# Raw weight loads moved ahead of the chunk loads, scaled queries moved behind x, and weights prepared at three of five places

## The chip, the cores and the metric

The kernel runs on one core of one Trainium2 chip. The metric is the device time of one launch in microseconds (us). Besides TensorE (PE), which multiplies, the core has VectorE (DVE), ScalarE (ACT), GpSimd (POOL), and SyncE (SP), which here only issues transfers (DMAs) from memory. Each engine works through its instructions in program order; an instruction that waits holds up those behind it on its engine.

## The reference, cut to what matters

```python
# 1. decaying linear attention, blocks of 64 positions, 2 batches x 8 heads x 768 positions x 64
for b in range(nb):
    intra = (einsum('bhic,bhjc->bhij', qb, kb) * Dmask) @ vb
    inter = einsum('bhid,bhde->bhie', qb * lam_pow, kv_state)
    out[:, :, sl] = intra + inter
    kv_state = lam_block * kv_state + einsum('bhsd,bhse->bhde', kb * rev_pow, vb)
x = out.transpose(0, 2, 1, 3).reshape(1536, 512)
# 2. gated layer: d_model 512, d_ff 1536
xn = x / sqrt(mean(x * x) + 1e-06) * rms_g
g = xn @ w_gate
x = (silu(g) * (xn @ w_val)) @ w_out
# 3. maxout layer: d_ff 768
h = maximum(maximum(x @ w1, x @ w2), x @ w3)
return h @ w_out2
```

All numbers are 32-bit floats. A product of two matrices is made as three products of their high and low parts, so each weight is split once into `wh` and `wl`.

## The kernel before, in words

**Attention** goes by chunks of 128 positions, 12 in all (c = 0 to 11). A chunk passes through steps, each a letter: `T` (`turn`: transposes of k and q on PE into the banks `pk` and `pq`, copies `kT` and `qT` on ACT, and the scaled queries `qs` on DVE, which read `pq`), `K` or `k` (decayed keys `kd`, POOL), `C` (`scores`, PE), `a` and `b` (masked scores `A` and the states `S`, DVE), `V` (state, DVE), `M` (`mixed`: PE makes `px`, ACT its squares `sq` and the copy `x`), `U` (`summed`: PE `pm`, DVE `diag`, POOL the power), `N` (`normed`: PE `pb`, DVE `x`, ACT `xh`) and `R` (POOL `xl`). The strings in `orders` fix the order of the steps in a round; in round s step `T` works on chunk s, `C` on s-1, `M` on s-2, `N` on s-3. From chunk 5 on the squares are first added up on DVE (`zeros` in the rows, line 394), and `pm` reads that sum.

**Rounds 0 to 6** run by themselves, in the loop at the end of the program. From round 3 on each of them also prepares one weight.

**The first stage** (`first_stage`) then multiplies with the first four column blocks f = 0 to 3 of the gated layer, for three blocks j of 512 positions. Its unit of order is a **place**: each three matmuls of 128x512 are followed by one call of `spread`, which may run one third of a weight's preparation (`third_of_unit`) and some attention steps. `pg` and `pv` of one f have four places each, the sum over two f's (`out_two`, `acc`) eight. For j = 0: `pg` and `pv` of f = 0 are places 1 to 8, of f = 1 places 9 to 16, `pg` of f = 2 is 17 to 20, `out_two` over f = 0, 1 is 21 to 28, `pv` of f = 2 29 to 32, f = 3 33 to 40; then `pg` of the next block, 41 to 44, and `out_two` over f = 2, 3, 45 to 52.

**A weight's way.** One raw weight of 512 KB comes by DMA into a buffer `wraw` (`load_to`; one DMA for an out weight `o`, three for a gate `g` or value `v`). Then ACT makes `W` and shifts the low words (lines 252, 253), DVE makes `mid` twice and `W` (209, 212, 216), POOL adds the low words (219); a unit later ACT makes `wh` (180) and POOL `wl` (183). The raw buffers are few: of the first ten loads three in five use one of three buffers, the others one of two; the later ones all use the three. A load whose buffer is still being read waits on SP, and every load behind it waits too, since all of them stand in SP's one queue.

```python
if not lates and (pos["half"] - 1) % 4:      # spread: three places of four
    third_of_unit()
load_to(pos["raw"] + (3 if pos["half"] else 1))   # begin_unit
```

In the order of use the weights are g0, v0, g1, v1, g2, o0, o1, v2, g3, v3, o2, o3, and then g4, v4 and on, which the first stage doesn't need. Raw loads are counted from 0, so g4 is number 12 and v4 number 13.

**The second stage** does the rest of the gated layer and the maxout layer, with weights prepared at three of four gaps.

Of the kernel before, what the change touches and what calls it, by code (L numbers as in the profile page):

```python
# [9 lines left out]
F32 = mybir.dt.float32  # L10
# [8 lines left out]
P = 128  # L19
# [7 lines left out]
def tile_decay_attention_swiglu_maxout(  # L27
# [17 lines left out]
    B, H, S, D = q.shape  # L45
# [7 lines left out]
    C = P // 2  # L53
# [4 lines left out]
    NCH = NT // P  # L58
    CPNB = NB // P
# [9 lines left out]
    lates = []  # L69
# [161 lines left out]
    def begin_unit():  # L231
        if pos["made"] == len(unit_list):
            return
        key = unit_list[pos["made"]]
        at = group_of[key] % 2
        if first_use[key] <= pos["step"] + 6 and at < len(wpools) and (key is None or room[at]):
            pos["made"] += 1
            if key is None:
                stage1.append((None,) * 5)
                return  # L240
            room[at] -= 1
            held[key] = at
            if key[0][0] == "T":
                stage1.append((key, None if second_sum(key) else words[key[0][1], key[1]], at, None, None))
                return
            load_to(pos["raw"] + (3 if pos["half"] else 1))
            pos["raw"] += 1
            t = raws.pop(key).rearrange("p k (f w) -> p (k f) w", w=2)
            lo, hi = t[:, :, 0], t[:, :, 1]
            W = wp.tile([P, 512], I32, tag="W", name="W", bufs=4)  # L250
            words[key] = W
            nc.scalar.activation(out=W.bitcast(F32), in_=hi.bitcast(F32), func=AF.Abs)  # L252
            nc.scalar.activation(out=lo, in_=lo.bitcast(U32), func=AF.Copy, scale=2.0 ** -29)  # L253
            stage1.append((key, W, at, lo, hi))
# [32 lines left out]
        nc.gpsimd.tensor_tensor(out=kd[r], in0=qkv[c][0][r], in1=Tm[r, :, C - 1:C].to_broadcast([r.stop, H, D]),  # L287
                                op=ALU.mult)

    def turn(c):  # L290
        kn, qn, vn = qkv[c][0], qkv[c][1], qkv[c][2]
        pk = bank("pk")
        pq = bank("pq")
        pkv = pk.rearrange("p (a t) -> p a t", t=P)
        pqv = pq.rearrange("p (a t) -> p a t", t=P)
        for a in range(NP):
            nc.tensor.transpose(pkv[:, a, :], kn[:, 2 * a:2 * a + 2, :].rearrange("p h d -> p (h d)"), ident)
        for a in range(NP):
            nc.tensor.transpose(pqv[:, a, :], qn[:, 2 * a:2 * a + 2, :].rearrange("p h d -> p (h d)"), ident)
        kT = att.tile([P, NP, P], F32, tag="kT", name="kT", bufs=1)  # L300
        nc.scalar.copy(out=kT, in_=pkv)
        qT = att.tile([P, NP, P], F32, tag="qT", name="qT", bufs=1)
        nc.scalar.copy(out=qT, in_=pqv)
        qs = att.tile([P, NP, 2, C], F32, tag="qs", name="qs")
        h0 = 0 if c % CPB else 1
        nc.vector.tensor_tensor(
            out=qs[:, :, h0:], in0=pqv.rearrange("p a (h i) -> p a h i", h=2)[:, :, h0:],
            in1=lami.rearrange("p a (h i) -> p a h i", h=1).to_broadcast([P, NP, 2 - h0, C]), op=ALU.mult)
        if c == 0:
            decayed_keys(0)  # L310
        A = att.tile([P, H, C], F32, tag="A", name="A", bufs=1)
        st[c] = dict(kT=kT, qT=qT, qs=qs, vn=vn, A=A)

    def scores(c):
        d = st[c]
# [14 lines left out]
    def masked(hf):  # L330
        def piece(c):
            d = st[c]
            nc.vector.tensor_tensor(
                out=d["A"].rearrange("p (a t) i -> p t a i", t=2)[:, hf],
                in0=d["sc"][hf][:, :HF].rearrange("p (a i) -> p a i", i=C),
                in1=Tm.rearrange("p (a t) i -> p t a i", t=2)[:, hf], op=ALU.mult)
            if hf == 0:
                d["S0"] = last_state[0]
                d["S1"] = next_state(c, 0, d["S0"])
        return piece  # L340
# [82 lines left out]
    def rest(c):  # L423
# [5 lines left out]

    named = dict(M=(2, mixed), N=(3, normed), C=(1, scores), a=(1, masked(0)), R=(3, rest),  # L430
                 b=(1, masked(1)), U=(2, summed), V=(1, advance), T=(0, lambda c: (loads_at(c), turn(c))),
                 K=(-1, decayed_keys), k=(0, decayed_keys),
                 w=(3, lambda c: None))
    orders = ["MNCabUVTRK"] * (CPNB + 1) + ["MNCabUVTR", "MNCRabUkVT"] + ["MNCaUkRbVT"] * (NCH - CPNB - 2) + ["MNwRwU", "wwwNwR"]
    attn_q = [(s_, named[ch][1], s_ - named[ch][0]) for s_ in range(NCH + 3) for ch in orders[s_]
              if (ch == "K") <= s_ - named[ch][0] < NCH]
    gaps = [0, 0]
# [1 line left out]
    def attn_step():  # L439
        _, fn, c = attn_q.pop(0)  # L440
        fn(c)
# [16 lines left out]

    def spread():
        pos["half"] += 1  # L460
        if not lates and (pos["half"] - 1) % 4:
            third_of_unit()
        if gaps[0]:
            left = sum(1 for p in attn_q if p[0] <= gaps[1])
            for _ in range(-(-left // gaps[0])):
                attn_step()
            gaps[0] -= 1
            if not attn_q and not lates:
                att_ctx.close()
                wpools.append(ctx.enter_context(tc.tile_pool(name="wp2", bufs=8)))  # L470
                lates.append(ctx.enter_context(tc.tile_pool(name="late", bufs=1)))
                pos["narrow"] = False
                x_sums()
        if pos["half"] == 1:
            finish_unit(*stage2.pop(0))
            words_of_unit(3, *split_unit[0])
# [479 lines left out]
    with tc.manual_schedule():  # L956
        nc.scalar.dma_start(out=lam8, in_=lam.rearrange("(o h) -> o h", o=1).to_broadcast([P, H]))
        loads_to(0)
        for to, src in crosswise(g_sb, rms_g.rearrange("(a p) -> p a", p=P)):
            nc.scalar.dma_start(out=to, in_=src)  # L960
        make_identity(nc, ident)
        nc.vector.memset(ones, 1.0)
        nc.vector.memset(zeros, 0.0)
        nc.scalar.activation(out=mhalf, in_=zeros[:, 0:1], func=AF.Silu)
        nc.vector.memset(mhalf, -0.5)
        warm = bank("warm")
        for i in range(9):
            nc.tensor.matmul(out=warm[:, 0:P], lhsT=zeros, rhs=zeros, start=True, stop=True)
        nc.vector.tensor_tensor(out=diag, in0=ident[:, :C], in1=ident[:, C:], op=ALU.add)
        for hf in range(2):  # L970
            nc.vector.tensor_copy(out=lamh[64 * hf:64 * hf + 64, :],
                                  in_=lam8.rearrange("p (a t) -> p t a", t=2)[64 * hf:64 * hf + 64, hf, :])
        for a in range(NP):
            nc.vector.tensor_tensor_scan(
                out=lami[:, a, :], data0=lamh[:, a:a + 1].to_broadcast([P, C]), data1=zeros[:, :C],
                initial=1.0, op0=ALU.mult, op1=ALU.add)
        for h in range(H):
            nc.vector.tensor_tensor_scan(
                out=Tm[:, h, :], data0=lam8[:, h:h + 1].to_broadcast([P, C]), data1=diag,
                initial=0.0, op0=ALU.mult, op1=ALU.add)  # L980
        loads_to(1)
        pos["narrow"] = False
        unit_ = None
        for s_ in range(CPNB + 3):
            while attn_q[0][0] == s_:
                fn = attn_q[0][1]
                attn_step()
                if s_ > 2 and fn is named["N"][1]:
                    begin_unit()
                    unit_ = stage1.pop(0)  # L990
                if unit_ and s_ == CPNB + 2:
                    if fn is named["U"][1]:
                        words_of_unit(3, *added_later)
                    elif fn is named["V"][1]:
                        for n in range(3):
                            words_of_unit(n, *unit_, split_add=True)
                        split_unit.append(unit_)
                        stage2.append(unit_[:3])
                elif unit_ and fn is named["b"][1]:
                    words_of_unit(0, *unit_)  # L1000
                elif unit_ and fn is named["U"][1]:
                    words_of_unit(1, *unit_)
                    if stage2:
                        finish_unit(*stage2.pop(0))
                elif unit_ and fn is named["V"][1]:
                    words_of_unit(2, *unit_, split_add=s_ == CPNB + 1)
                    added_later = unit_
                    stage2.append(unit_[:3])
            if s_:
                load_to(pos["load"] + 1)  # L1010
        begin_unit()
        finish = first_stage()
        pos["step"] = len(steps)
        second_stage(finish)
# [31 lines left out]
```

## Time and profile before

| | |
|---|---|
| median of 3 runs | 547.11 us (546.27 to 547.93) |
| profiled execution | 548.3 us, of which the span is 546.5 us |
| PE busy | 531.0 us, 97% of the span |
| DVE, ACT, POOL busy | 371.7, 279.7, 300.9 us |
| DMA, first 110 us | 160 GB/s, DMA engines busy 64% |
| PE busy, first 110 us | 97.75 us |
| PE busy, from 110 us to 546 us | 433.27 of 436 us |

"Busy" is the sum of an engine's instructions. The granted TensorE clock is given as a share of full speed: 1.00 is 2.4 GHz, 0.5 is 1.2 GHz.

### The profile page before, as it was taken

How to read it: one execution, taken by the hardware profiler on the slowest of the kernel's cores; microseconds unless marked ns; L12 is line 12 of the kernel's file. 1: busy time of each engine (PE TensorE's matmuls, PEld its weight loads, DVE VectorE, ACT ScalarE, POOL GpSimd, SP SyncE). 2: the span in 40 equal slices, each digit the busy share in tenths (PEclk: the TensorE clock that was granted, in tenths of full speed). 3: DMA queues.
4: the chain of work that ended last, by engine and by line, in shares of the span. 5: the costliest groups of instructions: out<-in, count | busy, mean ns of one | idle time of the engine just before them, and what ended most of it. 6: DMA issues, size and time to landing. Idle time of an engine off the chain costs nothing.

```text
span 546.5 us, 9743 instructions
## 1 busy us (share of the span) xinstructions
PE 531.0 (97%) x3728; PEld 438.2 (80%) x3728; DVE 371.7 (68%) x680; ACT 279.7 (51%) x541; POOL 300.9 (55%) x247
## 2 busy tenths in 40 slices
PE   8998988999999999999999999999999999999997
PEld 7776756788888888888888888888888888888886
DVE  4776775545967676768677575887777477684464
ACT  3667674336264565464447426646466755651120
POOL 2485886241436486385556636886287544962050
PEclk9979999999999999999999999999999999999999
DMA  8888817000202132131221221121123222200015
GB/s 191 203 209 235 213 40 186 9 2 0 78 0 63 54 116 68 49 115 40 77 88 65 78 57 60 40 77 40 38 79 114 85 75 75 82 34 0 0 44 188
DMA packets 65598, 44.67 MB, mean 82 GB/s; under 512 B 40080, under 2 KB 61840, under 8 KB 65552
## 3 DMA queue, kind: packets, MB, share of 16 engines
q1 hardware_dynamic: 64848, 44.05, 28.4%
q8 instruction: 29, 0.48, 0.4%
q14 instruction: 17, 0.14, 0.1%
q10 hardware_dynamic: 704, 0.01, 0.1%
HBM read 40.90 MB, written 3.15 MB: 81 GB/s over the span
## 4 chain that ended last, share of the span: by engine, by line
PE 85%; DMA 4%; issue 2%; POOL 2%; SPq 2%; DVE 2%; ACT 2%; POOLq 0%; ACTq 0%; DVEq 0%
PE p L683 34%; PE acc L874 9%; PE r L683 8%; PE acc L480 6%; PE acc L482 6%; PE acc L481 6%; PE pv L490 5%; PE q L683 4%; PE pg L490 4%; DMA wraw<-in_moe_w_val_dram 3%; SPq L170 2%; PE px L377 1%; POOL W L219 1%; DMA qn<-in_q_dram 1%; PE sc L326 1%
## 5 line engine op out<-in xcount | busy, mean ns | idle before, releaser
L183 POOL TENSOR_TENSOR wl<-W,wh 128x512 fp32r<-128x512 f32 x77 | 100.7, 1309 | 60.5 <-ACT wh L180 60.5
L219 POOL TENSOR_TENSOR W<-W,wraw 128x512 int32<-128x512 int32 x60 | 80.6, 1343 | 71.9 <-DVE W L216 61.7
L180 ACT CAST wh<-W 128x512 fp32r<-128x512 f32 x77 | 47.8, 621 | 80.3 <-POOL W L219 78.8
L501 POOL TENSOR_TENSOR hl<-sg,hh 128x512 fp32r<-128x512 f32 x36 | 47.2, 1311 | 34.3 <-ACT hh L500 34.3
L683 PE MATMUL p<-xl,wh 128*128 128x512 f32 x148 | 57.6, 389 | 0.0
L683 PE MATMUL p<-xh,wl 128*128 128x512 f32 x148 | 57.6, 389 | 0.0
L683 PE MATMUL p<-xh,wh 128*128 128x512 f32 x148 | 57.6, 389 | 0.0
L480 PE MATMUL acc<-hh,wh 128*128 128x512 f32 x144 | 56.8, 394 | 0.7 <-DVE W L216 0.7
L481 PE MATMUL acc<-hl,wh 128*128 128x512 f32 x144 | 56.2, 390 | 0.0
L482 PE MATMUL acc<-hh,wl 128*128 128x512 f32 x144 | 56.1, 390 | 0.0
L252 ACT ACTIVATE W<-wraw 128x512 f32<-128x512 f32 x60 | 40.3, 672 | 9.9 <-DMA wraw<-in_moe_w_dram 4.4
L838 DVE TENSOR_TENSOR acc_sb<-acc,acc_sb 128x512 f32<-128x512 f32 x46 | 31.7, 690 | 19.5 <-PE acc L482 18.3
L209 DVE TENSOR_SCALAR mid<-W 128x512 f32<-128x512 f32 x58 | 39.8, 686 | 6.1 <-ACT W L252 6.1
L212 DVE TENSOR_SCALAR mid<-mid 128x512 int32<-128x512 int32 x58 | 40.3, 694 | 0.8
L216 DVE SCALAR_TENSOR_TENSOR W<-wraw,mid 128x512 int32<-128x512 int32 x58 | 39.5, 682 | 1.1
L253 ACT ACTIVATE wraw<-wraw 128x512 int32<-128x512 uint32 x60 | 39.9, 665 | 0.0
L738 ACT COPY c<-p 128x512 f32<-128x512 f32 x34 | 20.0, 587 | 38.3 <-PE p L683 38.3
L501 POOL TENSOR_TENSOR hl<-m,hh 128x512 fp32r<-128x512 f32 x18 | 24.2, 1350 | 23.0 <-ACT hh L500 23.0
L683 PE MATMUL p<-yl,wh 128*128 128x512 f32 x90 | 35.0, 389 | 0.0
L683 PE MATMUL p<-yh,wh 128*128 128x512 f32 x90 | 35.0, 389 | 0.0
L683 PE MATMUL p<-yh,wl 128*128 128x512 f32 x90 | 35.0, 389 | 0.0
L500 ACT CAST hh<-sg 128x512 fp32r<-128x512 f32 x36 | 22.3, 619 | 22.8 <-DVE sg L624 16.8
(176 smaller groups left out, 1322.9 us busy)
## 6 DMA issues: line engine op xcount, KB each, us to landing
wraw<-in_moe_w_out_dram SPq DMA_DIRECT2D x18, 512.0 KB, 3.4
wraw<-in_moe_w_dram SPq DMA_DIRECT2D x18, 512.0 KB, 3.5
kn<-in_k_dram SPq DMA_DIRECT2D x12, 256.0 KB, 4.3
qn<-in_q_dram SPq DMA_DIRECT2D x12, 256.0 KB, 4.7
vn<-in_v_dram SPq DMA_DIRECT2D x12, 256.0 KB, 4.9
wraw<-in_moe_w_gate_dram SPq DMA_DIRECT2D x12, 256.0 KB, 3.0
wraw<-in_moe_w_gate_dram SPq DMA_DIRECT2D x24, 128.0 KB, 3.3
wraw<-in_moe_w_val_dram SPq DMA_DIRECT2D x12, 256.0 KB, 3.0
```

The source lines that it names most:

```text
L180: nc.scalar.copy(out=wh, in_=W.bitcast(F32))
L183: nc.gpsimd.tensor_tensor(out=wl, in0=W.bitcast(F32), in1=wh.bitcast(F32), op=ALU.subtract)
L212: nc.vector.tensor_scalar(out=mid[key], in0=mid[key], scalar1=0x07FFFFFF, scalar2=3, op0=ALU.bitwise_and, op1=ALU.logical_shift_left)
L219: nc.gpsimd.tensor_tensor(out=W, in0=W, in1=lo, op=ALU.add)
L252: nc.scalar.activation(out=W.bitcast(F32), in_=hi.bitcast(F32), func=AF.Abs)
L480: nc.tensor.matmul(out=out, lhsT=wh, rhs=xh_, start=first, stop=False)
L481: nc.tensor.matmul(out=out, lhsT=wh, rhs=xl_, start=False, stop=False)
L482: nc.tensor.matmul(out=out, lhsT=wl, rhs=xh_, start=False, stop=last)
L490: nc.tensor.matmul(out=ps, lhsT=w[:, kk * P:(kk + 1) * P], rhs=x[:, kk, :], start=n == 0, stop=n == len(todo) - 1)
L501: nc.gpsimd.tensor_tensor(out=dst_l, in0=src, in1=dst_h.bitcast(F32), op=ALU.subtract)
L683: nc.tensor.matmul(out=ps, lhsT=w[:, ks], rhs=r[:, o + k, :], start=first and k == 0 and n == 0, stop=k == 1 and n == 2, skip_group_check= ...
L874: nc.tensor.matmul(out=acc[:, cs], lhsT=x[:, ts], rhs=w[:, cs], start=n == 0, stop=n == len(todo) - 1)
```

## The change

Four edits. In rounds 1 to 6 the round's raw load is issued before the step `T` and so before that round's chunk loads, instead of at the round's end. In the first stage a weight that is begun still asks for raw loads up to two ahead, but no further than number 12 (g4), so that v4 (13) is not asked for there. In rounds 1 to 6 the scaled queries are a step of their own, `Q`, which works on the chunk of the round before, behind `N` (and so behind `x`); from round 6 on `T` makes them itself as before. And thirds of a weight run at places 2, 3 and 5 of each five, no more at three of four, so the k-th weight's last part (`finish_unit`) stands at place 5k+3 instead of 4k+3: o1 at 18 for 15, v3 at 33 for 27, o2 at 38 for 31, o3 at 43 for 35. The tile `A` is now taken where it is first written.

```diff
-            load_to(pos["raw"] + (3 if pos["half"] else 1))
+            load_to(min(pos["raw"] + 3, 3 * PLAIN + 1) if pos["half"] and not lates else pos["raw"] + (3 if lates else 1))
...
-    def turn(c):
+    def turn(c, scaled=True):
...
+        st[c] = dict(kT=kT, qT=qT, pq=pqv, vn=vn)
+        if scaled:
+            scaled_queries(c)
+        if c == 0:
+            decayed_keys(0)
+
+    def scaled_queries(c):
+        pqv = st[c].pop("pq")
         qs = att.tile([P, NP, 2, C], F32, tag="qs", name="qs")
         h0 = 0 if c % CPB else 1
         nc.vector.tensor_tensor(
...
+        st[c]["qs"] = qs
...
+                 t=(0, lambda c: (loads_at(c), turn(c, False))), Q=(1, scaled_queries),
...
-    orders = ["MNCabUVTRK"] * (CPNB + 1) + ["MNCabUVTR", "MNCRabUkVT"] + ["MNCaUkRbVT"] * (NCH - CPNB - 2) + ["MNwRwU", "wwwNwR"]
+    orders = ["MNQCabUVtRK"] * (CPNB + 1) + ["MNQCabUVtR", "MNQCRabUkVT"] + ["MNCaUkRbVT"] * (NCH - CPNB - 2) + ["MNwRwU", "wwwNwR"]
...
-        if not lates and (pos["half"] - 1) % 4:
+        if not lates and (pos["half"] - 1) % 5 % 3:
             third_of_unit()
...
+                if s_ and fn in (named["t"][1], named["T"][1]):
+                    load_to(pos["load"] + 1)
                 attn_step()
...
-            if s_:
-                load_to(pos["load"] + 1)
```

PE's order is the same in both kernels, row for row. The other engines' orders change as these three places show.

SP's queue in rounds 4 to 6, before: v of chunk 5, k and q of chunk 6, the raw weight v1, v of chunk 6, the raw weight g2, and chunk 7.

```order
L92 DMA vn_600<-in_v_dram 128x8x64
L92 DMA kn_602<-in_k_dram 128x8x64
L92 DMA qn_604<-in_q_dram 128x8x64
L170 DMA wraw_626<-in_moe_w_val_dram 128x2x256
L170 DMA wraw_626<-in_moe_w_val_dram 64x2x256 x2
L92 DMA vn_741<-in_v_dram 128x8x64
L170 DMA wraw_761<-in_moe_w_gate_dram 128x2x256
L170 DMA wraw_761<-in_moe_w_gate_dram 64x2x256 x2
L92 DMA kn_863<-in_k_dram 128x8x64
```

The same loads in the changed kernel:

```order
L170 DMA wraw_600<-in_moe_w_val_dram 128x2x256
L170 DMA wraw_600<-in_moe_w_val_dram 64x2x256 x2
L92 DMA vn_604<-in_v_dram 128x8x64
L92 DMA kn_606<-in_k_dram 128x8x64
L92 DMA qn_608<-in_q_dram 128x8x64
L170 DMA wraw_741<-in_moe_w_gate_dram 128x2x256
L170 DMA wraw_741<-in_moe_w_gate_dram 64x2x256 x2
L92 DMA vn_745<-in_v_dram 128x8x64
L170 DMA wraw_863<-in_moe_w_out_dram 128x1024
```

Each raw weight has moved ahead of three chunk loads, and each chunk load behind one more raw weight than before; g0, v0 and g1 have moved likewise, and so have o0 and chunk 7.

SP's queue around chunk 10, before: the raw weights o3, g4 and v4, then chunk 10 and chunk 11.

```order
L170 DMA wraw_1316<-in_moe_w_out_dram 128x1024
L170 DMA wraw_1392<-in_moe_w_gate_dram 128x2x256
L170 DMA wraw_1392<-in_moe_w_gate_dram 64x2x256 x2
L170 DMA wraw_1433<-in_moe_w_val_dram 128x2x256
L170 DMA wraw_1433<-in_moe_w_val_dram 64x2x256 x2
L92 DMA kn_1442<-in_k_dram 128x8x64
L92 DMA qn_1444<-in_q_dram 128x8x64
L92 DMA vn_1446<-in_v_dram 128x8x64
```

The same in the changed kernel, where v4 comes only behind chunk 11:

```order
L170 DMA wraw_1378<-in_moe_w_out_dram 128x1024
L92 DMA kn_1417<-in_k_dram 128x8x64
L92 DMA qn_1419<-in_q_dram 128x8x64
L92 DMA vn_1421<-in_v_dram 128x8x64
L170 DMA wraw_1444<-in_moe_w_gate_dram 128x2x256
L170 DMA wraw_1444<-in_moe_w_gate_dram 64x2x256 x2
L92 DMA kn_1611<-in_k_dram 128x8x64
```

Chunk 10 has moved ahead of the two raw weights g4 and v4.

ACT's queue from `turn` of chunk 9 to the squares of chunk 8, before (`wh_1470` is that of v3):

```order
L301 COPY kT_1458<-pk_1448 128x512
L303 COPY qT_1460<-pq_1449 128x512
L642 COPY acc_sb_1380<-acc_1421 128x512
L180 CAST wh_1470<-W_1318 128x512
L388 ACTIVATE sq_1510<-px0_1475 128x256
L388 ACTIVATE sq_1510<-px1_1476 128x256
L390 ACTIVATE x_1511<-px0_1475,g_sb_75 128x128 x2
```

The same in the changed kernel (`W_1448` is that of o2, `wh_1500` that of g3):

```order
L301 COPY kT_1433<-pk_1423 128x512
L303 COPY qT_1435<-pq_1424 128x512
L650 COPY acc_sb_1366<-acc_1403 128x512
L252 ACTIVATE W_1448<-wraw_1254 128x512
L253 ACTIVATE wraw_1254<-wraw_1254 128x512
L395 ACTIVATE sq_1488<-px0_1453 128x256
L395 ACTIVATE sq_1488<-px1_1454 128x256
L397 ACTIVATE x_1489<-px0_1453,g_sb_75 128x128 x2
L397 ACTIVATE x_1489<-px1_1454,g_sb_75 128x128 x2
L180 CAST wh_1500<-W_1256 128x512
```

No `wh` stands between the copies of `turn` and the squares any more; it comes behind `x`. At `turn` of chunk 8 it is the same: before, the `wh` of o1 stands right ahead of `kT`; now it stands far behind `qT`.

## Rows read from the trace of the kernel before

**Rows 1.** Windows: stretch, length, busy PE, PEld, DVE, ACT, POOL; PEclk, DMA, GB/s.

```profile
0.00:110.00 110.00, 97.75 (x1752) 79.35 (x1752) 73.95 (x200) 64.75 (x150) 65.17 (x65) 0.97 0.64 160
110.00:546.00 436.00, 433.27 (x1978) 358.83 (x1977) 297.75 (x481) 215.00 (x392) 235.73 (x182) 1.00 0.20 62
...
24.20:31.20 7.00, 5.66 (x148) 4.94 (x148) 6.04 (x20) 5.36 (x13) 6.02 (x7) 0.93 0.85 210
31.20:38.50 7.30, 7.19 (x131) 6.27 (x132) 5.72 (x19) 5.09 (x13) 5.48 (x6) 0.60 0.84 202
```

**Rows 2.** Waits of PE, 0 to 110 us: in total, times, longest.

```profile
PE pk L297 <- DMA kn<-in_k_dram: 1.5, 1, 1.5
PE sc L321 <- ACT x L390: 1.4, 1, 1.4
PE pm L403 <- DVE zeros L394: 1.2, 3, 0.6
PE px L377 <- ACT sg L621: 1.1, 1, 1.1
...
PE pb L416 <- DVE mid L212: 1.1, 1, 1.1
PE acc L480 <- DVE W L216: 0.7, 1, 0.7
...
PE pb L416 <- ACT kT L301: 0.5, 1, 0.5
PE pq L299 <- DMA qn<-in_q_dram: 0.3, 1, 0.3
```

**Rows 3.** Timeline of SP: start, length, and what it issues.

```profile
84.16 1.67 SPq L170 DMA_DIRECT2D wraw<-in_moe_w_val_dram  x3
85.92 0.54 SPq L92 DMA_DIRECT2D kn<-in_k_dram  x1
```

**Rows 4.** Timeline of ACT; in brackets the idle time before, and its releaser.

```profile
40.02 0.68 ACT L252 ACTIVATE W<-wraw 128x512 f32<-128x512 f32 x1 [2.20 <-DMA wraw<-in_moe_w_val_dram]
...
64.32 0.62 ACT L180 CAST wh<-W 128x512 fp32r<-128x512 f32 x1 [1.55 <-POOL W L219]
64.84 0.58 ACT L301 COPY kT<-pk 128x512 f32<-128x512 f32 x1
...
79.88 0.62 ACT L180 CAST wh<-W 128x512 fp32r<-128x512 f32 x1 [1.60 <-POOL W L219]
80.40 0.65 ACT L388 ACTIVATE sq<-px 128x256 f32<-128x256 f32 x2
```

**Rows 5.** q of chunk 6: issue on SP, time to landing, first transpose on PE.

```profile
29.75 1.79 SPq L92 DMA_DIRECT2D qn<-in_q_dram  x1
...
DMA to landing us min/median/max: 6.4/6.4/6.4
...
39.02 0.60 PE L299 MATMUL pq<-ident,qn 128*128 128x128 f32 x4
```

**Rows 6.** Last wl of the first stage on POOL (o3); ACT idle behind.

```profile
93.01 1.28 POOL L183 TENSOR_TENSOR wl<-W,wh 128x512 fp32r<-128x512 f32 x1
...
98.42 0.62 ACT L420 CAST xh<-x 128x512 fp32r<-128x512 f32 x1 [0.71 <-DVE x L418]
104.63 0.58 ACT L301 COPY kT<-pk 128x512 f32<-128x512 f32 x1 [5.59 <-PE pk L297]
```

**Rows 7.** PE's timeline: matmuls ending places 33, 35, 43; first uses of v3, o3.

```profile
85.58 0.39 PE L490 MATMUL pg<-xh,wl 128*128 128x512 f32 x1
86.94 0.39 PE L490 MATMUL pg<-xh,wl 128*128 128x512 f32 x1
90.84 0.48 PE L490 MATMUL pv<-xh,wh 128*128 128x512 f32 x1
97.38 0.40 PE L490 MATMUL pg<-xl,wh 128*128 128x512 f32 x1
100.42 0.48 PE L480 MATMUL acc<-hh,wh 128*128 128x512 f32 x1
```

More of the change, by code (lines that the diff above doesn't have):

```diff
@@ L308, in turn @@
             in1=lami.rearrange("p a (h i) -> p a h i", h=1).to_broadcast([P, NP, 2 - h0, C]), op=ALU.mult)
[L309 to L312, printed above, removed]
+        st[c]["qs"] = qs
     def scores(c):
@@ L332, in piece @@
             d = st[c]
+            if hf == 0:
+                d["A"] = att.tile([P, H, C], F32, tag="A", name="A", bufs=1)
             nc.vector.tensor_tensor(
```

## The prediction

> **What bounds the kernel now.** I read the windows first. From 110 us to 546 us PE is busy 433.27 of 436 us, and the list of waits names none of PE there: that stretch is PE's own work, and since PE's order is the same row for row in both kernels, the change can shorten it by nothing. Up to 110 us PE is busy 97.75 us [rows 1]. So some 12 us of idle time is all there is to win, and what a slower clock costs. Second, the list of PE's waits in that stretch says who ends them [rows 2]: chunk 10's k and q landing late (1.5 and 0.3 us), a bank that ACT frees late for `sc` (1.4) and for `pb` (0.5), the sum of squares for `pm` (1.2 in three waits), a bank freed by the Silu (1.1), the power for `pb` (1.1, in round 5), and a bank freed by DVE's `W` (0.7): 7.8 us. The rest, some 3 us, is the start, where nothing changes. Third, for each of these I looked on the timeline of the named engine at what stood ahead of it.
>
> Two things come out. ACT and SP wait in order, for weights that are not urgent, with urgent work behind. On ACT the `wh` of a weight waits 1.55 us for POOL with `kT` of chunk 8 behind it, and the `wh` of v3 waits 1.60 us with the squares of chunk 8 behind it; in round 6 ACT waits 2.20 us for the raw weight v1 [rows 4]. On SP the raw weight v4 is issued at 84.16 us, when its buffer comes free, and chunk 10, needed at once, follows at 85.92 us [rows 3].
>
> Between 24 and 38.5 us the DMA engines are 84 to 85% busy at 202 to 210 GB/s, and TensorE's granted clock, in tenths of full speed, means 0.93 and then 0.60, so part of it ran at 1.2 GHz instead of 2.4: (1 - 0.93) x 2 x 7.0 + (1 - 0.60) x 2 x 7.3 = 6.8 us at half clock [rows 1].
>
> **The change, part by part.** The sum is made against the profiled execution, 548.3 us with a span of 546.5 us; that is 1.2 us above the median of 547.11 us, and I take the same difference off the median.
>
> *Chunk 10 ahead of g4 and v4.* What held the queue was v4's buffer. Now o3 stands ahead of chunk 10, and its buffer is that of o1, read long before; g4 behind it is not urgent. Chunk 10 can go as soon as o3 has gone, and both waits go: **-1.8 us** [rows 2, 3]. Bounds: 1.5 if only the first went, 1.8.
>
> *No `wh` ahead of `kT` and the squares.* By the order, `wh` of o1 and v3 have moved behind the copies of `turn` and behind `x`. ACT is then at `kT` of chunk 8 without the 1.55 us and the 0.62 us of the `wh` [rows 4]; the 0.5 us at `pb` goes. Ahead of the squares of chunk 8 now stand two operations, each as long as the 0.68 us one in these rows, in place of 1.60 + 0.62 us, and they wait for no engine, so that they lie in time in which ACT was idle. So the 1.4 us at `sc` goes for the most part: I take 1.2, with bounds 0.6 and 1.4. Together **-1.7 us** [rows 2, 4].
>
> *`pm`.* Its sums come from ACT's squares, which stand behind the same weights on ACT: behind raw weights that land earlier now, and behind a `wh` that now follows them. Of 1.2 us I take **-0.9**, three quarters, since one wait may have another cause (bounds 0 and 1.2) [rows 2].
>
> *Rounds 3 to 6.* A raw weight of 512 KB takes 0.524 MB / 202 GB/s = 2.6 us of the DMA engines, three chunk loads of 256 KB 3.9 us [rows 1]. So each raw weight lands 3.9 us earlier, and ACT's wait of 2.20 us, and those like it that made `pb` 1.1 us late, go [rows 2, 4]. But each k and q lands 2.6 us later, and PE pays for that. What decides is q of chunk 6, which ends these rounds. It was issued at 29.75 us and landed 6.4 us later, at 36.15; now that is about 38.75, while PE began its transposes at 39.02 [rows 5]. PE gets there earlier, then waits for q6 instead. So of the 1.1 us, and of the half clock too, only 39.02 - 38.75 = **-0.3 us** comes through (bounds: -1.1 if the DMA engines run freer; +1.5 if q6 lands 1.8 us later still). `x` ahead of `qs` on DVE lets ACT's `xh` start one DVE operation earlier in each round, in this same slack: nothing.
>
> *What stays.* The Silu behind the `wh` of v1 (1.1) and the bank that `W` frees (0.7) [rows 2] stand in the same order as before: nothing, at best -1.8.
>
> *Weights at three of five.* No work is taken away; it is spread over more places, and the last weights come later against PE. The tightest is o3. Its `wh` stood at place 35 and its `wl` ended at 93.01 + 1.28 = 94.29 us; PE first uses the weight at 100.42, and its `wl` two matmuls later, at about 101.0 [rows 6, 7]. Now `finish_unit` stands at place 43, which PE ends at 97.38 + 0.40 = 97.8 us. ACT has just one cast ahead of it there, `xh`, which ended at 99.04, and is then idle for 5.59 us: `wh` 99.04 to 99.66, `wl` to 100.94 [rows 6]. That meets the 101.0 with nothing to spare: **+0.3 us**. Bounds: 0, and 3.8 if the weight lags as far behind its place as before. (Before, PE ended place 35 at 86.94 + 0.39 = 87.3, so `wl` came 7.0 us behind; 97.8 + 7.0 = 104.8, less 101.0 is 3.8 [rows 6, 7].)
>
> *From 110 us on:* the second stage begins its weights some places earlier or later, PE covers it all, as it covers everything now [rows 1]: nothing.
>
> Sum: -1.8 - 1.7 - 0.9 - 0.3 + 0.3 = **-4.4 us**: 548.3 becomes 543.9, and the median 547.1 becomes **542.7 us**.
>
> **The rivals.** A measurement of this kernel tells about 0.3%, 1.6 us, from no change.
>
> *The clock falls at a worse time.* A round's loads take 2.6 + 3.9 = 6.5 us, where PE was busy for 5.66 us in a round at nearly the full clock [rows 1]; so PE will idle in rounds 4 to 6, waiting for k and q, some 0.8 us in each, or all of it before chunk 6. Before, the half clock came in the round with an idle of 1.1 us, and ran 6.8 us under work that the DMA engines bounded anyway [rows 1, 2]. If it falls instead as PE leaves round 6, the 6.8 us lie under dense work and cost half, 3.4 us: 542.7 + 3.4 = 546.1, no difference. For it: more idle time than before. Against it: the fall before came by 31 us (0.93 is one microsecond of half clock in the stretch that ends at 31.2), and the idle time there is of the same size [rows 1]. The Trainium skill, "TensorE: Matmul & The Clock Gate", section "Part 1: The HAM clock gate", says that the array is throttled by default and that activity releases it; by that rule the added idle time speaks against this change, and the time would be this rival's. The trace agrees so far that the only long stretch at half clock lies in the rounds in which PE waits.
>
> *ACT's waits only move.* POOL is as loaded as before up to the second f, and `wh` waits for it elsewhere with other urgent work behind. Then of the second and third terms nothing comes: 542.7 + 1.7 + 0.9 = 545.3, just faster. For it: the work is the same. Against it: the order shows nothing urgent behind `wh` at the two places.
>
> *The late weights stop PE (slower).* If v3 and o3 both lag 7.0 us behind their places, as o3 did: v3's place 33 ends at 85.58 + 0.39 = 86.0, so `wl` comes at 93.0; PE wants it half a microsecond into `pv`, at 90.84 + 0.5 = 91.3, less the 1.8 us that no longer pass before it: 89.5. That is 3.5 us of waiting, and o3 makes 3.8 [rows 6, 7]. So -4.4 - 0.3 + 7.3 = +2.6: 549.7 us. For it: nothing in the first stage has more than a few us to spare in the new order. Against it: the lag of o3 was that of a queue behind late hidden halves, and from 99 us on ACT is idle. It decides at the lag where the two waits, (lag - 3.5) + (lag - 3.2), reach the gain of 4.7 us: 5.7 us.
>
> **How the numbers follow.** Forecast as summed, 541 to 544.5: 0.62. More goes (the Silu, the bank, `pb`), 540 to 541: 0.07. ACT's waits only move, 545.3: 0.10, which lies at the edge of 0.3% (545.5), so I count half as faster. Clock, 546.1: 0.11. Late weights, 549.7, or half of that: 0.10. Faster 0.62 + 0.07 + 0.05 = 0.74; the same 0.05 + 0.11 and a little of the late weights, 0.17; slower 0.09. The range leaves out the best ends of all terms below 540.0 and most of the late weights above: 540.0 to 546.8.
>
> **What would show it.** Right: no wait of PE for k or q of chunk 10, and chunk 10 issued well before 84 us; ACT's squares of chunk 8 start at once behind `px`; in round 6 ACT waits for no raw weight, and PE waits for q of chunk 6 and begins to transpose it at about 38.8 us; PE meets 110 us some 4 us ahead in its rows. Wrong: PE idle before the first `acc` of o3 or in `pv` of v3; granted clock at half behind 39 us; or PE at chunk 6 later than 40 us, which means that the DMA engines and not ACT set the rounds by more than I reckon. Waits of PE behind 110 us would say that the second stage has less cover than its rows show.

## The result and the profile after

The changed kernel takes 540.1 us (median of 4 runs, 539.56 to 540.95), the kernel before 546.78 us on the same chip (4 runs, 546.27 to 547.93): a ratio of 0.9876, 95% interval 0.9855 to 0.9898, thus 6.7 us faster. The forecast was 542.7 us with a range from 540.0: the direction held, and 2.3 us more came than the sum said. The profiled executions stand 7.35 us apart (548.3 and 540.95 us; spans 546.5 and 539.2).

The windows of the changed kernel, with the columns of [rows 1]; the last stretch is one in which the clock was low.

```profile
0.00:110.00 110.00, 102.00 (x1842) 83.21 (x1843) 76.81 (x209) 66.96 (x157) 68.26 (x68) 0.97 0.64 160
110.00:539.00 429.00, 426.05 (x1888) 352.92 (x1886) 293.12 (x472) 211.27 (x385) 233.03 (x179) 1.00 0.20 63
...
38.10:41.50 3.40, 3.39 (x39) 2.49 (x39) 2.15 (x4) 2.09 (x4) 2.69 (x3) 0.50 0.97 248
```

The mean clock, DMA share and GB/s of the first 110 us are as before [rows 1]; PE is busy for 102.00 us there in place of 97.75. PE's waits in that stretch, as in [rows 2] (left out are those of the start, and two in the rounds, of 1.0 and 0.8 us, for which the profile names no engine):

```profile
PE pq L299 <- DMA qn<-in_q_dram: 0.6, 2, 0.4
PE acc L490 <- POOL wl L183: 0.5, 1, 0.5
PE px L384 <- ACT sg L629: 0.3, 1, 0.3
PE sc L331 <- DMA vn<-in_v_dram: 0.2, 1, 0.2
```

The waits for k of chunk 10, for `x`, for the sums of `pm`, for `mid`, for `W` and for `kT` are gone; the Silu's is down from 1.1 to 0.3 us; one for a `wl` is new. The chunks show where the time went. PE begins the transposes of chunk 6 at 38.55 us before and 37.10 after, of chunk 7 at 47.98 and 47.56, of chunk 8 at 60.92 and 59.12, of chunk 9 at 73.71 and 71.08, of chunk 10 at 89.50 and 82.23, of chunk 11 at 103.94 and 96.61. From chunk 10 on the lead is 7.3 us, and it is 7.3 us at the end of the span: behind the first stage nothing came and nothing went.

SP in the changed kernel (columns as in [rows 3]): first q of chunk 6, then o3, k of chunk 10 and g4.

```profile
31.66 2.91 SPq L92 DMA_DIRECT2D qn<-in_q_dram  x1
...
64.60 0.34 SPq L170 DMA_DIRECT2D wraw<-in_moe_w_out_dram  x1
65.03 0.39 SPq L92 DMA_DIRECT2D kn<-in_k_dram  x1
...
69.37 1.68 SPq L170 DMA_DIRECT2D wraw<-in_moe_w_gate_dram  x3
```

Chunk 10 is asked for at 65.03 us, 17 us ahead of its transposes; in [rows 3] it was 85.92, behind v4.

ACT in the changed kernel, at the two places of [rows 4]: `kT` of chunk 8, then the squares of that chunk.

```profile
59.32 0.62 ACT L180 CAST wh<-W 128x512 fp32r<-128x512 f32 x1 [1.74 <-POOL W L219]
59.84 0.59 ACT L629 ACTIVATE sg<-pg 128x512 f32<-128x512 f32 x1
60.33 0.58 ACT L301 COPY kT<-pk 128x512 f32<-128x512 f32 x1
...
74.35 0.68 ACT L395 ACTIVATE sq<-px 128x256 f32<-128x256 f32 x2
74.88 1.17 ACT L397 ACTIVATE x<-px,g_sb 128x128 f32<-128x128 f32 x4
75.87 0.69 ACT L180 CAST wh<-W 128x512 fp32r<-128x512 f32 x1
```

The squares begin with no wait ahead of them and the `wh` comes behind `x`. A `wh` that waits for POOL still stands two instructions ahead of `kT` (it is o0's, 1.74 us), but it starts at 59.32, as PE begins to transpose chunk 8 (59.12), so nobody waits for it.

### The profile page after: what moved, and what is told of

The parts are those of the page before. It is cut to its first block, busy times and chain, and to the rows that moved or that the text cites. A ratio compares the mean times of both kernels' runs of the same rounds, so it can differ in the third digit from the quotient of the medians.

```text
span 539.2 us, 9762 instructions
## 1 busy us (share of the span) xinstructions
PE 528.1 (98%) x3728; PEld 436.1 (81%) x3728; DVE 369.9 (69%) x680; ACT 278.2 (52%) x541; POOL 301.3 (56%) x247
## 4 chain that ended last, share of the span: by engine, by line
PE 84%; DVE 1%; POOL 0%; issue 0%; ACT 0%; DVEq 0%
PE p L691 34%; PE acc L882 9%; PE r L691 9%; PE acc L488 6%; PE acc L490 6%; PE acc L489 6%; PE pv L498 5%; PE q L691 4%; PE pg L498 4%; PE px L384 1%; POOL wl L183 0%; PE sc L326 0%; PE sc L331 0%; PE pb L423 0%; DVE S L358 0%
## 5 line engine op out<-in xcount | busy, mean ns | idle before, releaser
L183 POOL TENSOR_TENSOR wl<-W,wh 128x512 fp32r<-128x512 f32 x77 | 102.1, 1326 | 53.1 <-ACT wh L180 53.0
L219 POOL TENSOR_TENSOR W<-W,wraw 128x512 int32<-128x512 int32 x60 | 79.1, 1318 | 75.9 <-DVE W L216 75.6
L746 ACT COPY c<-p 128x512 f32<-128x512 f32 x34 | 19.9, 586 | 38.0 <-PE p L691 37.7
```

Of the source, the lines that this page charges most:

```text
L183: nc.gpsimd.tensor_tensor(out=wl, in0=W.bitcast(F32), in1=wh.bitcast(F32), op=ALU.subtract)
L219: nc.gpsimd.tensor_tensor(out=W, in0=W, in1=lo, op=ALU.add)
```

## The experiments

"T(7) to T(10)" is the time from the first transposes of chunk 7 to those of chunk 10, from the profile: 41.5 us before, 34.7 after. Ratios are to the kernel before, measured with each group on its chip (medians 545.84, 547.13 and 546.57 us). The first four kernels have one edit each.

**The raw loads ahead, alone.**

```diff
+                if s_ and fn is named["T"][1]:
+                    load_to(pos["load"] + 1)
                 attn_step()
...
-            if s_:
-                load_to(pos["load"] + 1)
```

> Only the raw load ahead of the chunk loads in rounds 1 to 6. Pace theory (the gain comes from fewer weights in ACT's, POOL's and DVE's way in the first stage): 0.3 to 0.8 us less than before, about 546.3, because PE then waits for q of chunk 6 instead of for the power; the waits behind 48 us stay. Load theory (the gain comes from raw weights that land earlier): 2.5 us less or more, about 544.3, and the wait of px for the Silu falls from 1.1 us to below 0.5.

545.37 us, ratio 0.9991 (0.9974 to 1.0007): no difference. T(7) to T(10) 40.7 us. The wait for the Silu fell to 0.3 us; a wait for q of chunk 6 of 1.6 us came at 37.63 us. That is what the forecast said of rounds 3 to 6: q lands later and takes back what the weights give. The fall of the Silu's wait was to speak for the load theory, but no time came with it.

**The limit on the lookahead, alone.**

```diff
-            load_to(pos["raw"] + (3 if pos["half"] else 1))
+            load_to(min(pos["raw"] + 3, 3 * PLAIN + 1) if pos["half"] and not lates else pos["raw"] + (3 if lates else 1))
```

> Only the limit on how far ahead raw weights are asked for in the first stage: g4 still stands ahead of chunk 10, v4 no more. Pace theory: the 1.8 us of PE's waits for k and q of chunk 10 go and no other, about 545.0. Load theory: 3 us less, about 543.8, since what stood behind late chunk loads comes earlier too.

542.1 us, ratio 0.9937 (0.9921 to 0.9952), thus -3.4 us (-2.6 to -4.3); T(7) to T(10) 39.1 us, 2.4 less. Its waits of PE from 40 to 110 us:

```profile
PE sc L321 <- ACT x L390: 1.5, 1, 1.5
PE acc L480 <- DVE W L216: 0.7, 1, 0.7
PE pm L403 <- DVE zeros L394: 0.6, 2, 0.3
PE pb L416 <- ACT kT L301: 0.5, 1, 0.5
PE px L377 <- ACT sg L621: 0.3, 1, 0.3
```

Those for chunk 10 are gone; those for `x`, `W` and `kT` are as in [rows 2]. The time is the load theory's, the waits are the pace theory's: matmul by matmul, the kernel before falls 2.20 us behind this one at chunk 10, where its two waits sum to 1.8, and nothing more is won behind it. The rest of the 3.4 us is not shown to come from the edit. Nor are the smaller waits for the Silu (0.3 for 1.1 us) and the sums (0.6 for 1.2): they end well ahead of 84 us, where SP before issues v4 [rows 3], and up to there the two kernels have the same instructions in the same order on every engine.

**The scaled queries behind `x`, alone.**

```diff
-    orders = ["MNCabUVTRK"] * (CPNB + 1) + ["MNCabUVTR", "MNCRabUkVT"] + ["MNCaUkRbVT"] * (NCH - CPNB - 2) + ["MNwRwU", "wwwNwR"]
+    orders = ["MNQCabUVtRK"] * (CPNB + 1) + ["MNQCabUVtR", "MNQCRabUkVT"] + ["MNCaUkRbVT"] * (NCH - CPNB - 2) + ["MNwRwU", "wwwNwR"]
```

> Only the scaled queries behind x. Both theories: no change, 546.8 within 0.5 us. If x reaching ACT one DVE operation earlier mattered, the wait of pb in round 5 (1.1 us) would fall and the time by about 1 us.

545.11 us, ratio 0.9995 (0.9979 to 1.0012); T(7) to T(10) 41.5 us. As expected, nothing.

**Three of five, alone.**

```diff
-        if not lates and (pos["half"] - 1) % 4:
+        if not lates and (pos["half"] - 1) % 5 % 3:
```

> Only thirds of a weight at three of five places; this alone already puts chunk 10 ahead of g4 and v4 on SP. Pace theory: the waits of PE for ACT's x, for kT, for the bank of W, and for chunk 10 go: about 5 us less, 541.8, and what is left to the full change is below 2 us. Load theory: only chunk 10's 1.8 us, about 545.0. If late weights cost, PE waits for wl of o1 or o3 by 0.5 us or more each.

538.8 us, ratio 0.9879 (0.9859 to 0.9898): the whole gain of the change, and more than the 5 us of the pace theory; T(7) to T(10) 35.5 us. By this edit alone chunk 10 comes ahead of g4 and v4 on SP, since the weights that ask for those are begun later. All its waits of PE from 40 to 110 us:

```profile
PE px L377 <- ACT sg L621: 1.1, 1, 1.1
PE acc L482 <- POOL wl L183: 0.5, 1, 0.5
```

**All but the pace.** The change with its last edit undone (`% 5 % 3` back to `% 4`).

> The three other edits together, weights still at three of four places. Rate theory (the slower pace gives nearly the whole gain, and of the others only the limit on the lookahead counts): as the limit alone, 0.994 of before, some 542.5 us, range 541.3 to 543.5; PE still waits some 1.4 us for ACT's x ahead of sc in the first stage. Rival (the raw weights ahead and the late scaled queries add something once chunk 10 is no longer in the way): 541.0 us or less. The record of the prediction has -1.8 and -0.3 for these parts, thus some 543.7.

544.18 us, ratio 0.9941 (0.9918 to 0.9964), the same as the limit alone; PE waits 1.5 us for `x`, 0.7 for `W`, 0.5 for `kT`. The two other edits add nothing.

What is it in the pace: that ACT, DVE and POOL have less to do in a place, or on which place each piece falls? Four kernels ask this.

**Three of four at other places, with the limit** (whose edit is the one shown above).

```diff
-        if not lates and (pos["half"] - 1) % 4:
+        if not lates and pos["half"] > 1 and pos["half"] % 4:
```

> The limit on the lookahead, and three of four places still, but the place without a third is the fourth of each four and not the first. Rate theory: the helpers have as much to do in a place as before, so the waits of sc for x and of pb for kT stay or move to other rows; as the limit alone, 542.5 us, range 541.5 to 543.8. Rival (phase: what counts is only which place a wh falls on against kT and the squares): moving all of them by up to a place takes the waits away or makes them worse, 540.5 us or less, or 544.5 or more.

546.96 us, ratio 1.0007 (0.9991 to 1.0023). The time is the phase rival's: the gain of the limit is lost, though chunk 10 isn't waited for. The first waits of PE from 40 to 110 us:

```profile
PE pb L416 <- POOL xl L428: 2.5, 1, 2.5
PE pm L403 <- DVE zeros L394: 1.5, 1, 1.5
PE sc L321 <- ACT x L390: 1.4, 1, 1.4
```

At three of four, then, the places do count: the waits move and may grow. The longest is the forecast's wait for `kT` under another name. `pb` takes the bank that `pk` had, which is free when ACT has made `kT`; `xl`, which the list names, merely ends close to that. POOL and ACT ahead of it:

```profile
62.62 1.06 POOL L287 TENSOR_TENSOR kd<-kn,Tm 128x512 f32<-128x512 f32 x1
63.64 1.28 POOL L219 TENSOR_TENSOR W<-W,wraw 128x512 int32<-128x512 int32 x1
64.95 0.62 ACT L180 CAST wh<-W 128x512 fp32r<-128x512 f32 x1 [2.53 <-POOL W L219]
65.48 0.58 ACT L301 COPY kT<-pk 128x512 f32<-128x512 f32 x1
```

`kT` ends at 66.06 us and `pb` starts at 66.20, as much behind it as before (65.42 and 65.57). In the limit alone POOL makes this `W` ahead of `kd`; here `kd` comes first, the `wh` waits 2.53 us, and `kT` stands behind it.

**Three of five at places 3, 4 and 5.**

```diff
-        if not lates and (pos["half"] - 1) % 4:
+        if not lates and (pos["half"] - 1) % 5 > 1:
```

> Only the pace, at three of five places, but at places 3, 4 and 5 of each five and not 2, 3 and 5, so that each weight's last part stands at place 5k+4 and not 5k+3. Rate theory: the gain of the pace stays, less at most one place of 0.7 us for a weight that comes later against PE: 0.988 to 0.990 of before, 539 to 540.5 us. Rival (phase): the gain was one of coincidence with the places 2, 3 and 5, and 1.5 us of it or more go: 541 us and more.

545.01 us, ratio 0.9962 (0.9945 to 0.9979). The time is that of the rival, the profile is not: the waits for `x`, `kT` and `W` are gone here too, and PE is not behind the pace alone at chunk 8 (56.17 against 57.80 us). Nearly all is lost to weights that are one place later:

```profile
PE pv L490 <- POOL wl L183: 2.6, 1, 2.6
PE pm L403 <- DVE zeros L394: 1.0, 1, 1.0
PE acc L480 <- ACT wh L180: 1.0, 1, 1.0
PE acc L482 <- POOL wl L183: 0.6, 1, 0.6
```

The wait of 2.6 us in `pv` (that of v3) ends at 85.17 us. Behind it the granted clock falls; windows of this kernel around that wait:

```profile
82.10:85.10 3.00, 0.50 (x3) 0.07 (x1) 2.08 (x4) 1.27 (x3) 3.00 (x4) 1.00 0.01 3
86.60:90.00 3.40, 3.40 (x16) 2.19 (x19) 0.69 (x1) 1.00 (x2) 2.52 (x2) 0.50 0.56 151
```

From the matmul behind the wait to 91.3 us this kernel loses another 1.55 us against the pace alone.

**Four of seven.**

```diff
-        if not lates and (pos["half"] - 1) % 4:
+        if not lates and (pos["half"] - 1) % 7 in (1, 2, 4, 6):
```

> Only the pace, slower still: four thirds in seven places. The last parts then stand for o1 at place 19 for 18, v3 at 35 for 33, o2 at 40 for 38, o3 at 45 for 43. With three of five, wl of o1 came 0.5 us late and wl of v3 ended within 0.1 us of its first use. Late weights (each place later is 0.7 us of PE): o1 0.7 us more, v3 1.4, o3 0.5 to 1.4: in all 2.0 to 3.5 us above three of five, 541 to 542.5 us, with the waits of PE on wl of o1 and v3. Rival (ACT and POOL, with less to do, bring a weight earlier against its place, so that the lateness does not grow): 539.5 us or less.

546.63 us, ratio 0.9988 (0.9974 to 1.0002): the late weights, and more than was expected of them. PE waits 2.6 us for `wl` of v3 and 2.2 us in four waits for other `wl` and `wh`; from 88.0 us on 3.4 us run at a granted clock of 0.51.

**Three of five at places 2, 3 and 4.** The last part of each weight stands where the change has it; only DVE's `W` and POOL's sum stand a place earlier.

```diff
-        if not lates and (pos["half"] - 1) % 4:
+        if not lates and (pos["half"] - 1) % 5 in (1, 2, 3):
```

> Only the pace, three of five, at places 2, 3 and 4 of each five: the last parts stand at 5k+3 as in the change, so no weight comes later against PE; only DVE's W and POOL's sum stand at place 4 for 5. Rate theory: as the pace alone, 0.987 to 0.989 of before, with wl of o1 late by about 0.5 us and no wait for x, kT or W. Rival (the gain hangs on which place each operation falls on): a wait for a bank behind DVE's W, for kT or for x comes back, 0.990 or more.

538.54 us, ratio 0.9862 (0.9828 to 0.9896); T(7) to T(10) 34.95 us. PE's waits from 40 to 110 us:

```profile
PE px L377 <- ACT sg L621: 1.2, 1, 1.2
PE pm L403 <- DVE zeros L394: 0.7, 1, 0.7
```

None for `x`, `kT` or `W`, and none for `wl` of o1, which was expected. So in three arrangements of three of five, those waits are gone in each; what tells these apart is how late v3 and o1 come.

**The change at two of three** (`% 5 % 3` to `% 3`).

> The changed kernel with thirds at two of three places: last parts of o1 at place 17 for 18, v3 at 30 for 33, o3 at 39 for 43, thus a pace between the one before and the changed one. If the wait of PE for wl of o1 (0.5 us) and the lack of any reserve for v3 are all that three of five costs, and two of three still leaves the helpers their time: 0.5 us less than the changed kernel, 0.986 to 0.988. Rival (each step of the pace towards three of four brings a wh or a W back in front of kT, x or A): waits of PE for ACT or DVE of 1 us and more come back, 0.990 to 0.995, 541.5 to 544 us.

539.48 us, ratio 0.9881 (0.985 to 0.9911): not to be told from the change. The wait for `wl` of o1 is gone, and in its place are four short ones (0.52 for `x`, 0.30 for `S`, 0.34 for `xl`, 0.42 for `acc_sb`); T(7) to T(10) 36.7 us. The rival's waits come back, but small.

**The change without its first edit** (a round's raw load at the round's end again).

> The changed kernel without its first edit: a round's raw load stands behind its chunk loads again. In the profile of the changed kernel chunk 7 began at 47.56 us, with the pace alone at 45.45, and with raw loads ahead the wait for the Silu was 0.3 us in place of 1.1. Theory (with three of five, raw loads ahead give some 0.8 us at the Silu and cost about as much where k and q of the rounds come later): no difference to the changed kernel, 0.986 to 0.990 of before, 538.5 to 541 us. Rival 1 (raw loads ahead cost the 2 us of chunk 7): 0.984 or less, 538 us or less. Rival 2 (they are part of the gain): 0.991 or more.

538.57 us, ratio 0.9864 (0.9833 to 0.9895). Chunk 7 starts at 44.32 us, and the wait for the Silu is 1.1 us again. It is at most a little faster than the change; the intervals overlap, so neither it nor places 2, 3 and 4 is shown to beat the changed kernel.

## Why the forecast was right in kind and short in size

**The step that failed is "What stays", for the bank that `W` frees.** It gave this wait (0.7 us) as "in the same order as before: nothing". It went, and 0.9 us with it. What was left out is which bank of PE's results the waiting matmul takes. `mid` takes one from the same banks as `acc`, and DVE's `W` is the last to read it (`narrow` is off here):

```python
mid[key] = W if pos["narrow"] else psum.tile([P, 512], I32, tag="bank", name="mid")
```

By the order in which the kernel before takes its banks, this `acc` gets the one that `mid` of v3 had, and it starts as that `W` ends (first fence). With three of five one `mid` fewer is taken on the way, and the same `acc` gets the bank of an earlier `acc`, which ACT had copied out 2.2 us before (second fence):

```profile
74.69 0.69 DVE L216 SCALAR_TENSOR_TENSOR W<-wraw,mid 128x512 int32<-128x512 int32 x1
75.43 0.50 PE L480 MATMUL acc<-hh,wh 128*128 128x512 f32 x1 [0.69 <-DVE W L216]
```

```profile
69.04 0.58 ACT L650 COPY acc_sb<-acc 128x512 f32<-128x512 f32 x1
...
71.87 0.48 PE L488 MATMUL acc<-hh,wh 128*128 128x512 f32 x1
```

The limit alone and all but the pace leave the banks as before, and keep the wait of 0.7 us.

**The Silu's wait shrank as well, but that is no gain.** From the squares of chunk 5 to the Silu ACT takes 6.76 us before and 6.79 after, and 6.70 to 6.90 in all thirteen profiles. Before (first fence), then after:

```profile
43.72 0.65 ACT L388 ACTIVATE sq<-px 128x256 f32<-128x256 f32 x2
...
50.48 0.59 ACT L621 ACTIVATE sg<-pg 128x512 f32<-128x512 f32 x1
```

```profile
42.46 0.66 ACT L395 ACTIVATE sq<-px 128x256 f32<-128x256 f32 x2 [1.40 <-PE px L384]
...
49.25 0.59 ACT L629 ACTIVATE sg<-pg 128x512 f32<-128x512 f32 x1
```

What differs is when PE comes. In the changed kernel PE, which had just run 3.4 us at half clock, comes 1.05 us behind the end of the sums for the first `pm`; before, it waits 0.61 us for them. So what is won at this `pm` and at the Silu only hands back what PE had lost ahead of them. The limit alone shows the same two changes in the order of before, so the raw loads are not needed for it. For the Silu "nothing" was right.

**The terms were mis-sized in one way throughout: a wait costs more than its row says.** Two pieces of PE's timeline with the same matmuls show it, before and then after; a `pm` waited before.

```profile
56.48 0.40 PE L490 MATMUL pg<-xh,wl 128*128 128x512 f32 x1
57.20 0.35 PE L403 MATMUL pm<-ones,zeros 128*128 128x1 f32 x2 [0.32 <-DVE zeros L394]
57.41 0.47 PE L490 MATMUL pg<-xh,wh 128*128 128x512 f32 x1
```

```profile
55.24 0.39 PE L498 MATMUL pg<-xh,wl 128*128 128x512 f32 x1
55.47 0.28 PE L410 MATMUL pm<-ones,zeros 128*128 128x1 f32 x2
55.61 0.48 PE L498 MATMUL pg<-xh,wh 128*128 128x512 f32 x1
```

From `pg` to `pg` it is 0.93 us with the wait of 0.32 and 0.37 without: 0.56 us. Matmuls start 0.23 us apart but are shown 0.39 long, and a wait is counted only from the shown end. So this stop, when it goes, gives back 0.24 us more than its row. The same comparison, start by start, for each place where the two profiles drift apart:

| what | forecast, us | measured, us |
|---|---|---|
| k and q of chunk 10 (rows: 1.5 + 0.3) | -1.8 | -2.2 |
| `kT` (0.5) and `x` (1.4) | -1.7 | -0.8 - 1.8 = -2.6 |
| `pm`, second and third wait (0.3 each) | -0.4 | -0.57 - 0.55 = -1.1 |
| up to the Silu: q of chunk 6, half clock behind it, first `pm` (0.6), Silu (1.1) | -0.3 - 0.5 | -0.9 + 1.4 - 0.85 - 0.8 = -1.2 |
| bank of `W` (0.7) | 0 | -0.9 |
| late weights | +0.3 | +0.6 + 0.2 = +0.8 |
| two small drifts without a wait | | -0.4 |
| sum | -4.4 | -7.6 |

The forecast's -0.9 for `pm` is split here by the rows. The end of the span says -7.3. Against the forecast, 0.9 us of the miss is "What stays"; 0.4 + 0.9 + 0.7 = 2.0 are chunk 10, ACT's two waits and the later two of `pm`, for the most part six stops at some 0.2 us each and the parts that had been held back; 0.4 came up to the Silu and 0.4 in the small drifts; 0.5 goes the other way, to the late weights.

**Right, point by point.** *Chunk 10:* shown by the limit alone. In the change, though, the pace does the same by itself, so the two edits are one gain. *ACT's waits:* the mechanism held for `x`; at `kT` a `wh` still waits nearby, only earlier. There the banks changed too: `pb` takes one that DVE reads and no longer that of `pk`, so it would not have waited for `kT` in any case. That it is the pace which does it, and not the limit or the scaled queries, is shown by the single edits. *Rounds 3 to 6:* q of chunk 6 was forecast to land at 38.75 us; it took 6.3 us from its issue at 31.66, and PE began its transposes at 38.11, having waited 0.38 us, thus 0.9 us earlier than before and not 0.3. In kind the raw loads gave and took, as reckoned, and the edit alone gave nothing. *Behind 110 us:* PE is busy for 426.05 of 429 us and waits for nothing.

**The late weights** were the tight place, but the tightest was not o3. POOL's timeline of the changed kernel has the `wl` of o1, v3 and o3, and PE's the first matmul that reads each:

```profile
66.65 1.29 POOL L183 TENSOR_TENSOR wl<-W,wh 128x512 fp32r<-128x512 f32 x1 [0.82 <-ACT wh L180]
...
82.46 1.29 POOL L183 TENSOR_TENSOR wl<-W,wh 128x512 fp32r<-128x512 f32 x1
...
92.18 1.29 POOL L183 TENSOR_TENSOR wl<-W,wh 128x512 fp32r<-128x512 f32 x1 [1.39 <-ACT wh L180]
```

```profile
67.99 0.50 PE L490 MATMUL acc<-hh,wl 128*128 128x512 f32 x1 [0.53 <-POOL wl L183]
...
83.80 0.50 PE L498 MATMUL pv<-xh,wl 128*128 128x512 f32 x1
...
93.52 0.50 PE L490 MATMUL acc<-hh,wl 128*128 128x512 f32 x1
```

o3 ends at 93.47 and is read at 93.52: it meets PE with nothing to spare, as the forecast had it. v3 ends at 83.75 and is read at 83.80, 0.2 us behind the rhythm. o1, which the forecast didn't weigh, is 0.5 us late. So the rival of the late weights was one place away: at places 3, 4 and 5 PE waits 2.6 us for v3, of the rival's 3.5, though not for o3.

**The clock** fell for 3.4 us at 38.1 us, right behind PE's short wait for q of chunk 6, and cost 1.4 us: the place of that rival, with less than half of its 3.4 us. The other 3.4 us at half clock (0.50 from 21.05 to 24.45 us) lay in the rounds, so up to 110 us the changed kernel ran 6.8 us at half clock behind its start, as the kernel before did. The sentence cited for it from the Trainium skill ("TensorE: Matmul & The Clock Gate", "Part 1: The HAM clock gate"), that activity releases the clock, agrees with the falls to 0.50 and 0.51 behind the long waits for v3; it did not tell which side wins here.

**What stays open** is what in the pace removes the waits. All three kernels at three of five are without those for `x`, `kT` and `W`, and two of three has only short ones in between, which fits a lighter load per place. But no run changed the load without moving the pieces, and moving them changes what stands ahead of what on POOL and ACT, and which bank a matmul gets. For `W` the change of banks is cause enough, and for the 2.5 us at three of four the order on POOL; for `x` the load and the order are not told apart.

## What to carry to other kernels

Preparation that isn't urgent stands in the same in-order queues as work that is; spreading it thinner can remove many small waits at once, until the last part of one item meets its reader; behind that point one or two places cost most or all of what was won. When an order changes, look up each wait of the list in the new order of the engine that ends it, and also which bank the waiting matmul gets and who read that bank last, before writing "the same". Before a shorter wait is called a gain, look whether it differs as much between two kernels that are the same up to there. And price a vanished stop by the distance between the starts of the same instructions with and without it, not by the wait's row.

## What was not expected of the hardware

A wait of PE of 2.5 to 2.6 us was followed by a stretch of 3.4 us at half clock in all three profiles that had one: it ended at 85.17, 87.53 and 66.20 us, and the low stretches began at 86.6, 88.0 and 66.3. Against the pace alone, the two kernels with late weights lost 1.55 and 1.7 us more in that stretch, so that a late weight cost that much beyond its wait. Two waits of PE close together before (1.5 and 0.3 us for chunk 10) were followed by none. A shorter wait does not rule a fall out: with the scaled queries alone a stretch at 0.50 began at 80.0 us, behind a wait of 1.5 us for `x` that ended at 78.58, while the same wait in the kernel before (until 81.62) and in the limit alone (until 78.31) had none behind it.

In the rounds the low stretches come and go between kernels that are the same there: 30.3 us (6.8 us long) in the kernel before, 35.6 in the limit alone, 19.9 in three of five alone, none before 110 us in places 2, 3 and 4. With them chunk 7 starts anywhere from 44.3 to 48.0 us. Differences of a microsecond or two ahead of chunk 7 were therefore not put down to an edit.
